# Segment 0's x: two row loads for the first 256 tokens, one DMA transpose for the rest, and Q summed per token half

## The chip, the cores and the metric

The kernel runs on one core of a Trainium2 chip. The core has five engines that run side by side, each with its own queue of instructions: TensorE (PE) multiplies matrices, VectorE (DVE) and ScalarE (ACT) work on elements, GpSimd (POOL) does masks and small copies, and SyncE (SP) here only starts transfers (DMAs). In the profile PEld are TensorE's loads of the stationary operand, which overlap its matmuls. A matmul writes to PSUM, which has 8 banks of 512 fp32 columns by 128 partitions; all other on-chip data is in SBUF. The metric is the device time of one execution in microseconds, as the median of several runs.

## The reference, cut to what matters

Two blocks read the same x (2048 tokens of 512) and are mixed by a gate per token.

```
x = A_x
g = sigmoid((x * gate_w).sum(-1, keepdims=True))
a = A(x)          # attention over 4 segments of 512 tokens, 32 heads of 16, with a memory
b = B(x)          # ((x@W_gate) * (x@W_gate > 0) * (x@W_up)) @ W_down,  512 -> 1792 -> 512
return g * a + (1 - g) * b

# A, for each segment s (q, k, v are x@wq, x@wk, x@wv):
p     = softmax(qs @ ks.T * scale + causal mask)
a_mem = (phi(qs) @ M) / (phi(qs) @ z + 1e-6)      # phi(t) = t + 1 if t > 0 else exp(t)
o     = sigmoid(beta) * a_mem + (1 - sigmoid(beta)) * (p @ vs)
M, z  = M + phi(ks).T @ vs, z + sum(phi(ks))
# out of A: o @ wo
```

## The kernel before, in words

**Layout.** Tokens are handled in four segments of L = 512. All projections need x with its 512 features on the partitions: `xT[seg % 3]` holds one segment as 4 chunks (`ci`) of 128 features by 512 tokens. For Q and K, chunk `c` of the output (128 features, 8 heads) is the sum over the four `ci` of `wq_sb[:, ci, 128c:128c+128]` (stationary) with `xT[:, ci, :]` (moving); V has x stationary and `wv_sb` moving. The gated block makes 14 tiles of 128 hidden features with the gate weights (G, `wg_sb`) and the up weights (U, `wu_sb`), and the down projection (D, `wd_sb`) sums them, together with the attention's output through `wo_sb`, into one bank per 128 tokens.

**Array shapes.** TensorE works in three shapes: full matmuls (line 493), the same matmul as four pieces of 32 output columns (line 497, used where a stretch of work holds matmuls of that shape anyway), and four row groups of 32 for the scores (line 685). P times V (line 757) and the memory update (line 880) use the pieces of 32 columns, the recall of the memory uses 32 by 32 tiles (line 855).

**Attention.** One score group (`visit`) fills four banks, or up to seven, with scores; ScalarE takes their exponential in one instruction per up to four banks (line 714), which frees the banks; GpSimd masks (line 730).

**Order.** Every step is registered with `plan.add` in the order of the program text, with an engine, a duration, a key, and what it waits for. The durations and keys are what a planner once used; at build time nothing is planned. `Plan.run` takes the numbers in `ORDER`, a written-out list of all steps, and each engine's instructions are issued in that order. `UNITS` gives the bank or buffer of each slot. `LANDS` holds assumed arrival times of the first loads in ns. Waits between engines follow from data, whatever these numbers say. Step numbers in `ORDER` count the calls of `plan.add`, so adding a step renumbers all that come later.

**The opening.** The loads at the start are issued in program text order, outside the plan, by SyncE's queue (two by ScalarE's):

- `n0` (SyncE) and `n1` (ScalarE): the first 256 features of tokens 0 to 255 and 256 to 511, rows on partitions, into `xn`;
- `q0` (SyncE), `q1` (ScalarE): `wq` for chunks 0 and 1, 128 KB each;
- on SyncE then: `ka` (`wk` chunks 0 and 1, 256 KB), `wq` chunks 2 and 3 (256 KB, line 318), the DMA transpose of the other 256 features of all 512 tokens into `xT[0][:, 2:4, :]` (line 320), `kb`, `wv`, the first pieces of `wg` and `wu`, gate_w, beta, the second pieces, the rest of `xn` for the gate (`n2`), the transpose of x for segment 1 (line 287), and the third and fourth pieces.

Meanwhile `heat` (line 1006) runs six matmuls of 512 columns and one of 128 on constants. `x0_tasks` turns chunks 0 and 1 of x on TensorE: for each chunk and each pair of token tiles, two matmuls with the identity (line 531, 128 columns each), then one copy of 256 columns to `xT[0]`, on VectorE for the first pair and on ScalarE for the second (line 546). After the last of these a matmul on zeros (`junk`, line 540, 256 columns) stands in front of Q. `proj_q` for segment 0 adds chunk by chunk, one matmul of 512 columns each: chunks 0 and 1 wait for the copies, chunks 2 and 3 for the DMA transpose. `proj_k`'s first step (chunks 0 and 1) waits for the copies and `ka`, its second for the transpose and `kb`. `load_late`, `load_xn` and `load_xT` for later segments, and the small transposes of phi(K) into `pK` (line 622) are SyncE steps within the plan.

Of the kernel before, what the change touches and what calls it, by code (L numbers as in the profile page):

```python
# [12 lines left out]
P = 128  # L13
# [179 lines left out]
def kernel(  # L193
# [71 lines left out]
    def bank(slot):  # L265
        return ps[:, slot.i * L:(slot.i + 1) * L]
# [806 lines left out]
```

## Time and profile before

| | |
|---|---|
| median of 3 runs | 262.08 us (261.82 to 262.22) |
| the profiled execution's own time | 262.61 us |
| its span, first to last instruction | 260.9 us |
| TensorE busy | 254.1 us, 97% |
| VectorE / ScalarE / GpSimd busy | 202.1 / 183.0 / 67.3 us |
| TensorE's first matmul | 0.84 us |
| first matmul of Q | 4.57 us |
| first score group | 15.27 us |

A row of the timeline gives the start, the duration, the engine, the line, the operation, output and input, shapes, and how many instructions were merged; in brackets stands the idle time of the engine just before, and what ended it. Durations of matmuls are from entry to the last result, and neighbours overlap, so the rate of a series is read from the starts. A row of the table of stretches gives the stretch, its length, busy time of each engine with the number of instructions (PE, PEld, DVE, ACT, POOL), the granted TensorE clock, the share of the DMA engines and the GB/s they moved. A few per cent of the matmul records are missing from the trace.

### The profile page before, as it was taken

The numbers are of one execution on the slowest core, as the hardware profiler recorded it, in microseconds if no ns is written. First come the engines' busy times: TensorE is split into PE (matmuls) and PEld (weight loads), VectorE is DVE, ScalarE is ACT, GpSimd is POOL, SyncE is SP. The second block draws the span as 40 slices with busy tenths as digits, with TensorE's granted clock in tenths as the row PEclk, the third lists the DMA queues.
The fourth block names the chain that finished last, engine by engine and source line by source line (L and its number), as shares of the span: only waits on it lengthen the run. The fifth ranks groups of instructions, "written<-read, shape, count | busy, mean of one in ns | idle before, by whom it ended". The sixth has DMA issues, their size and how long they took to land.

```text
span 260.9 us, 9058 instructions
## 1 busy us (share of the span) xinstructions
PE 254.1 (97%) x3914; PEld 120.7 (46%) x3942; DVE 202.1 (77%) x452; ACT 183.0 (70%) x186; POOL 67.3 (26%) x188
## 2 busy tenths in 40 slices
PE   8999999999999999999999999999999999999995
PEld 3444444444545444454545444444545444445445
DVE  2499889999888957998998894697888736596622
ACT  3199899998889678797377837989477875793000
POOL 8018742224322213113021242124112422112000
PEclk9999999999999999999999999999999999999999
DMA  7999963030006243300016541000000043000011
GB/s 194 314 284 259 283 140 105 3 68 13 3 23 132 64 114 75 68 3 3 15 35 107 167 110 57 4 0 8 14 0 10 7 145 112 0 3 3 3 40 43
DMA packets 31600, 19.75 MB, mean 76 GB/s; under 512 B 16072, under 2 KB 30024, under 8 KB 31560
## 3 DMA queue, kind: packets, MB, share of 16 engines
q1 hardware_dynamic: 31144, 18.90, 28.6%
q8 instruction: 31, 0.51, 0.9%
q10 hardware_dynamic: 416, 0.26, 0.3%
q14 instruction: 9, 0.07, 0.1%
HBM read 13.21 MB, written 2.55 MB: 60 GB/s over the span
## 4 chain that ended last, share of the span: by engine, by line
PE 97%; issue 1%; DVE 0%
PE ps L493 53%; PE ps L497 25%; PE ps L685 9%; PE ps L757 7%; PE ps L1006 1%; PE ps L880 1%; PE ps L855 0%; PE ps L531 0%; PE ps L814 0%; DVE osr L961 0%; PE ps L540 0%
## 5 line engine op out<-in xcount | busy, mean ns | idle before, releaser
L714 ACT ACTIVATE E<-ps 128x2048 bf16<-128x2048 f32 (+3 forms) x79 | 120.4, 1552 | 26.4 <-PE ps L685 25.6
L730 POOL TENSOR_SCALAR_AFFINE_SELECT E<-E 128x256 bf16<-128x256 bf16 x128 | 53.7, 448 | 155.0 <-ACT E L714 149.1
L931 DVE TENSOR_TENSOR hT<-ps,rgr 128x512 bf16<-128x512 f32 x56 | 37.8, 681 | 21.9 <-PE ps L493 13.5
L925 ACT ACTIVATE rgr<-ps 128x512 bf16<-128x512 f32 x56 | 32.7, 596 | 20.3 <-PE ps L493 11.1
L493 PE MATMUL ps<-xT,wu_sb 128*128 128x512 bf16 x158 | 41.9, 380 | 0.6 <-issue 0.5
L493 PE MATMUL ps<-xT,wg_sb 128*128 128x512 bf16 x132 | 34.9, 379 | 0.6 <-issue 0.3
L493 PE MATMUL ps<-wd_sb,hT 128*128 128x512 bf16 (+2 forms) x147 | 29.5, 339 | 1.4 <-issue 1.3
L685 PE MATMUL ps<-QT,KT 32*128 32x64 bf16 (+3 forms) x768 | 27.8, 244 | 0.0
L788 DVE STREAM_TRANSPOSE T<-ps 128x512 f32<-128x512 f32 x32 | 21.9, 701 | 3.5 <-PE ps L757 3.1
L497 PE MATMUL ps<-wd_sb,hT 128*32 128x512 bf16 x384 | 24.0, 380 | 0.0
L493 PEld LDWEIGHTS <-wu_sb 128*128 128x128 bf16 x164 | 14.9, 98 | 18.5 <-issue 2.5
L497 PE MATMUL ps<-xT,wg_sb 128*32 128x512 bf16 x344 | 23.1, 380 | 0.0
L685 PEld LDWEIGHTS <-KT 32*128 32x128 bf16 x768 | 11.0, 92 | 24.1 <-issue 22.8
L961 DVE TENSOR_SCALAR osr<-ps,ngcol 128x512 bf16<-128x512 f32 (+2 forms) x18 | 12.2, 682 | 11.3 <-PE ps L493 10.4
L493 PEld LDWEIGHTS <-wg_sb 128*128 128x128 bf16 x138 | 12.9, 98 | 15.7 <-issue 1.3
L493 PEld LDWEIGHTS <-hT 128*128 128x128 bf16 x156 | 13.5, 98 | 14.1 <-issue 2.3
L757 PE MATMUL ps<-E,Vp 128*17 128x320 bf16 (+3 forms) x512 | 19.1, 273 | 0.0
L714 ACT ACTIVATE Em<-ps 128x2048 bf16<-128x2048 f32 (+2 forms) x11 | 15.6, 1415 | 4.3 <-PE ps L685 4.1
L497 PE MATMUL ps<-xT,wu_sb 128*32 128x512 bf16 x240 | 16.2, 379 | 0.0
L588 DVE CAST QT<-ps 128x512 bf16<-128x512 f32 x16 | 10.9, 684 | 6.0 <-PE ps L493 5.5
L493 PE MATMUL ps<-xT,wq_sb 128*128 128x512 bf16 x49 | 14.3, 407 | 0.2 <-issue 0.2
L493 PE MATMUL ps<-wv_sb,xT 128*128 128x512 bf16 x54 | 13.9, 379 | 0.4 <-issue 0.3
(100 smaller groups left out, 308.7 us busy)
## 6 DMA issues: line engine op xcount, KB each, us to landing
out_dram<-osr SPq DMA_DIRECT2D x15, 128.0 KB
xn<-in_A_x_dram SPq DMA_DIRECT2D x3, 512.0 KB
xn<-coefs SPq DMA_DIRECT2D x6, 256.0 KB
cdr<-coefs SPq DMA_DIRECT2D x6, 256.0 KB
wg_sb<-in_B_W_gate_dram SPq DMA_DIRECT2D x2, 512.0 KB
wu_sb<-in_B_W_up_dram SPq DMA_DIRECT2D x2, 512.0 KB
wd_sb<-in_B_W_down_dram SPq DMA_DIRECT2D x2, 512.0 KB
wg_sb<-in_B_W_gate_dram SPq DMA_DIRECT2D x2, 384.0 KB
```

Of the source, the lines that this page charges most:

```text
L493: nc.tensor.matmul(out, lhsT=lhsT, rhs=rhs, start=start, stop=stop)
L497: nc.tensor.matmul(out[r], lhsT=lhsT[:, r], rhs=rhs, start=start, stop=stop, tile_position=(0, 32 * j))
L588: prj["q", seg, c] = plan.add("DVE", 600, key - RQK, lambda: nc.vector.tensor_copy(QT[i][:], bank(sl)), [a] + war, DVL, frees=[sl])
L685: nc.tensor.matmul(ps[:, o:o + w], lhsT=lhsT.rearrange("p h q -> p (h q)"), rhs=rhs, start=True, stop=True, tile_position=(32 * j, 0))
L714: lambda n0=n0, n1=n1, u=u, f=f, j0=j0, j1=j1: nc.scalar.activation(target(u, f, j0, j1), ps[:, banks[n0] * L:(banks[n0] + n1 - n0) * L], ...
L730: nc.gpsimd.affine_select(out=m[:, :, o:o + HP], in_=m[:, :, o:o + HP], compare_op=ALU.is_ge, fill=0.0, base=HP, pattern=[[0, 4], [1, HP]] ...
L757: nc.tensor.matmul(bank(sl)[32 * m:32 * m + HW, q:q + w], lhsT=(Vp[i] if n < 4 else Vm)[:, kb, r, 4 * c + j, 0:HW], rhs=rhs, start=(n == 0 ...
L788: done.append(plan.add("DVE", 633, key - RL, lambda r=r, sl=sl: nc.vector.transpose(T[ts.i][:, r], bank(sl)), [a] + done, 75 if r else 0, ...
L880: nc.tensor.matmul(bank(sl)[32 * j:32 * j + 32, 34 * g:34 * g + 34], lhsT=pK[i][:, t, g * P + 32 * j:g * P + 32 * j + 32], rhs=Vp[i][:, t, ...
L925: r = plan.add("ACT", 478, key - RL, lambda sl=gsl, rs=rs: nc.scalar.activation(rgr[rs.i][:], bank(sl), ACT.Relu), [g], ACL, frees=[gsl])
L931: nc.vector.tensor_tensor(hT[hs1.i][:], bank(sl), rgr[rs.i][:], ALU.mult)),
L961: nc.vector.tensor_scalar(osr[os.i][:, n0 - c0:n1 - c0], bank(sl)[:, 0:n1 - n0], ngcol[:, tt:tt + 1], None, ALU.mult)),
```

## The change

Segment 0's x is split by tokens and no longer by features. Tokens 0 to 255 come as two loads of 128 whole rows, one from each queue; TensorE turns them chunk by chunk, one matmul of 128 columns and one copy of 128 columns for each of the 4 chunks and 2 token tiles, each in a bank of its own. Tokens 256 to 511 come by one DMA transpose of all 512 features. It is issued right after `wq`'s chunks 2 and 3; `ka` moves behind it. `n2` now loads tokens 256 to 511 as rows. Q of segment 0 is summed for the first 256 tokens with one matmul of 256 columns per chunk, each waiting for that chunk's two copies, and then for the second 256 tokens in two steps of two chunks, which wait for the transpose. Both steps of K wait for the transpose. The matmul on zeros and the last warming matmul of 128 columns are gone. Some values of `LANDS` differ, and `ORDER` and `UNITS` are written anew (1377 steps for 1362).

```diff
-    LANDS = dict(n0=3470, n1=3600, q0=4640, q1=4640, ka=6350, q2=7150, q3=7150, x0=8150,
-                 kb=9000, v=10600, g0=12100, u0=13600, gw=14100, be=14400, g1=15600, u1=17100,
+    LANDS = dict(n0=3250, n1=3300, q0=4100, q1=4100, q2=5100, q3=5100, x0=6300, ka=7100,
+                 kb=8000, v=9800, g0=11300, u0=12900, gw=14100, be=14400, g1=15600, u1=17100,
...
-    halves = slice(0, D // 2), slice(D // 2, D)
-    got_n[0] = [load_x0(eng, 2 * t, 2 * t + 2, halves[0], "n%d" % t)
+    got_n[0] = [load_x0(eng, t, t + 1, slice(0, D), "n%d" % t)
                 for t, eng in enumerate((nc.sync, nc.scalar))]
...
-    got_k = [load_rows(nc.sync, wk_sb, A_wk, 0, "k")]
     nc.sync.dma_start(out=wq_sb[:, 2:NC, :],
                       in_=A_wq.rearrange("(c p) n -> p c n", p=P)[:, 2:NC, :])
-    nc.sync.dma_start_transpose(out=xT[0][:, NC // 2:NC, :], in_=x[0:L, halves[1]])
+    got_q += [arrival("q%d" % ci) for ci in range(2, NC)]
+    nc.sync.dma_start_transpose(out=xT[0][:, :, 2 * P:L], in_=x[2 * P:L, :])
     got_x0b = arrival("x0")
-    got_q += [arrival("q%d" % ci) for ci in range(2, NC)]
+    got_k = [load_rows(nc.sync, wk_sb, A_wk, 0, "k")]
...
-    got_n[0].append(load_x0(nc.sync, 0, NC, halves[1], "n2"))
+    got_n[0].append(load_x0(nc.sync, 2, NC, slice(0, D), "n2"))
...
     def x0_tasks():
...
+        for ci in range(NC):
             for t in range(2):
+                sl = plan.one("ps", (2 * ci + t,))
+                a = plan.add("PE", 107, K(-9) + 2 * ci + t, lambda t=t, ci=ci, sl=sl: nc.tensor.matmul(
+                    bank(sl)[:, 0:P], lhsT=xn[:, t, ci * P:(ci + 1) * P], rhs=ident[:],
+                    start=True, stop=True), [got_n[0][t]], PEL, need=[sl], size=2)
...
+                x0_turned[ci].append(plan.add(
+                    "ACT" if t else "DVE", 80 + (0.95 if t else 1.12) * P, K(-9) + ci,
+                    lambda t=t, ci=ci, sl=sl: (nc.scalar.copy if t else nc.vector.tensor_copy)(
+                        xT[0][:, ci, t * P:(t + 1) * P], bank(sl)[:, 0:P]), [a], DVL, frees=[sl]))
+        return [x0_turned[k] + x0_turned[k + 1] + [got_x0b] for k in (0, 2)]
...
     # proj_q, segment 0
+            for ci in range(NC):
+                a = matmuls(K(-8 + ci, c), [got_q[ci]] + x0_turned[ci], sl, [
+                    lambda ci=ci: (wq_sb[:, ci, c * P:(c + 1) * P], xT[0][:, ci, 0:2 * P])],
+                    prev=a, start=not ci, stop=ci == NC - 1, width=2 * P)
+            a = matmuls(K(-3, c), [got_x0b], sl, [
+                lambda ci=ci: (wq_sb[:, ci, c * P:(c + 1) * P], xT[0][:, ci, 2 * P:L])
+                for ci in range(NC)], prev=a, width=2 * P, at=2 * P)
...
     def heat():
-        for k in range(7):
-            w = L if k < 6 else P
+        for k in range(6):
+            w = L
...
```

In the new order TensorE runs six flips, Q of c = 1 with chunk 0, the last two flips, the other fifteen Q matmuls of the first half, five steps of the second half, and then K, the rest of Q, V, the first G and the first score group. On SyncE the plan's steps begin with the transpose of x for segment 2, two of the `wd` loads, one `pK` transpose, three `wo` loads, `xn` of segment 1 and three more `pK` transposes; before, they began with two `pK` transposes, `xn` of segment 1, one `wo` and two `wd` loads, a `pK` transpose and the transpose for segment 2.

More of the change, by code (lines that the diff above doesn't have):

```diff
@@ L31 @@
 ORDER = """
[63 rows of a table removed]
[64 rows of a table added]
 """
 UNITS = (
[L98 to L104 removed]
+    "41635207000000005201073022171036330110330000030011000003011000001001030000210102218002d013"
+    "2120b302a0110301621042205200731132231320c1129010201002202122031210013132230003011303141321"
+    "230000000000320110000023000000000200112000072010007a32263001511c11293205301012071034000262"
+    "03211b313d12280002010210721110712362231131301222317111623520310000000001200100000340110000"
+    "00230112000032010606c5123321d3006213500140201102b1138026a313902027110201700020102407231116"
+    "22011303214307046371302000000000730000000031011000000330000000670102133605b211c61220037521"
+    "9120d02043001212a114821163020025501100011021"
 )
@@ L430 @@
     got_gates = plan.add("DVE", 300, 0.0, pair_gates, got_gates, 100, lock=True)
-    att, prj, ffn, xread, x0_first = {}, {}, {}, [], []
+    att, prj, ffn, xread, x0_turned = {}, {}, {}, [], [[] for _ in range(NC)]
     UNIT, AUNIT = 16000.0, 14800.0
@@ L523, in x0_tasks @@
         plan.tag = "x0"
-        got, prev = [], None
-        for ci in range(NC // 2):
+        prev = None
+        for ci in range(NC):
             for t in range(2):
-                sl = plan.one("ps", ((4, 3, 5, 2)[2 * ci + t],))
-                def flip(t=t, ci=ci, sl=sl):
-                    for k in range(2):
-                        nc.tensor.matmul(bank(sl)[:, k * P:(k + 1) * P],
-                                         lhsT=xn[:, 2 * t + k, ci * P:(ci + 1) * P], rhs=ident[:],
-                                         start=True, stop=True)
-                a = plan.add("PE", 214, K(-9 + ci) + t, flip, [got_n[0][t]], PEL, need=[sl], size=4)
+                sl = plan.one("ps", (2 * ci + t,))
+                a = plan.add("PE", 107, K(-9) + 2 * ci + t, lambda t=t, ci=ci, sl=sl: nc.tensor.matmul(
+                    bank(sl)[:, 0:P], lhsT=xn[:, t, ci * P:(ci + 1) * P], rhs=ident[:],
+                    start=True, stop=True), [got_n[0][t]], PEL, need=[sl], size=2)
                 if prev:
@@ L537, in x0_tasks @@
                 prev = a
-                if ci == 1 and t:
-                    js = plan.one("ps", (7,))
-                    j = plan.add("PE", 214, K(-9 + ci) + t, lambda js=js: nc.tensor.matmul(
-                        bank(js)[:, 0:2 * P], lhsT=junk[:, 0:P],
-                        rhs=junk[:, None, 0:P].to_broadcast([P, 2, P]), start=True, stop=True),
-                        [a], lat=0, need=[js], frees=[js], size=2)
-                b = plan.add(
-                    "ACT" if t else "DVE", 80 + (0.95 if t else 1.12) * P * 2,
-                    K(-9 + ci), lambda t=t, ci=ci, sl=sl: (
-                        nc.scalar.copy if t else nc.vector.tensor_copy)(
-                        xT[0][:, ci, 2 * t * P:2 * (t + 1) * P], bank(sl)[:, 0:2 * P]),
-                    [a], DVL, frees=[sl])
-                got.append(b)
-        x0_first.extend([got[0:2] + [(j, 0.0)], got[2:4]])
-        return [got, [got_x0b]]
+                x0_turned[ci].append(plan.add(
[3 more added lines that the diff above has]
+        return [x0_turned[k] + x0_turned[k + 1] + [got_x0b] for k in (0, 2)]
     def proj_mm(w, c, seg):
@@ L576, in proj_q @@
             a = None
-            for ci in range(2):
-                a = matmuls(K(-8 + ci, c), [got_q[ci]] + x0_first[ci], sl, [
-                    lambda ci=ci: (wq_sb[:, ci, c * P:(c + 1) * P], xT[0][:, ci, :])],
-                    prev=a, start=not ci, stop=False)
-            for ci in range(2, NC):
-                a = matmuls(K(-6 + ci, c), [got_q[ci]] + got_x[0][1], sl,
-                            [proj_mm(wq_sb, c, 0)[ci]], prev=a, start=False, stop=ci == NC - 1)
+            for ci in range(NC):
[5 more added lines that the diff above has]
+                for ci in range(NC)], prev=a, width=2 * P, at=2 * P)
         else:
@@ L1003, in heat @@
         one = nc.const_aps.tensor(1.0, (P, 1), BF16)
-        for k in range(7):
-            w = L if k < 6 else P
+        for k in range(6):
+            w = L
             nc.tensor.matmul(bank(warm[k])[:, 0:w], lhsT=one.to_broadcast([P, P]),
                              rhs=one.to_broadcast([P, w]), start=True, stop=True)
-    plan.add("PE", 3470, -1e9, heat, lat=0, need=warm, frees=warm, size=14)
+    plan.add("PE", 3363, -1e9, heat, lat=0, need=warm, frees=warm, size=12)
     got_x[0] = x0_tasks()
```

7 lines of the change are left out of this document (removed), and 127 rows, old and new, of the table ORDER.

## The prediction

> **What bounds the kernel now.** First I read the page's busy shares and the chain that ended last, then who waited for whom on TensorE.
>
> ```profile
> span 260.9 us, 9058 instructions
> PE 254.1 (97%) x3914; PEld 120.7 (46%) x3942; DVE 202.1 (77%) x452; ACT 183.0 (70%) x186; POOL 67.3 (26%) x188
> ...
> PE 97%; issue 1%; DVE 0%
> ```
>
> The chain is TensorE from end to end. Next, the timeline of TensorE: the opening, then the first attention scores (L685).
>
> ```profile
> 0.84 2.82 PE L1006 MATMUL ps<-const-bfloat16-1.0 128*128 128x512 bf16 x7 [0.84 <-PEq L1057]
> 3.50 1.04 PE L531 MATMUL ps<-ident,xn 128*128 128x128 bf16 x8
> 4.33 0.42 PE L540 MATMUL ps<-junk 128*128 128x256 bf16 x1
> 4.57 3.00 PE L493 MATMUL ps<-xT,wq_sb 128*128 128x512 bf16 x8
> 7.41 1.89 PE L493 MATMUL ps<-xT,wk_sb 128*128 128x512 bf16 x8
> 9.13 1.03 PE L493 MATMUL ps<-xT,wq_sb 128*128 128x512 bf16 x4
> ...
> 11.94 1.89 PE L493 MATMUL ps<-wv_sb,xT 128*128 128x512 bf16 x7
> ...
> 17.34 0.59 PE L493 MATMUL ps<-xT,wu_sb 128*128 128x512 bf16 x2
> 17.86 0.40 PE L685 MATMUL ps<-QT,KT 32*128 32x448 bf16 x8
> 18.19 0.60 PE L493 MATMUL ps<-wv_sb,xT 128*128 128x512 bf16 x2
> ```
>
> From 7.41 on, eight 512-column matmuls take 9.13-7.41 = 1.72 us, 0.215 each. The first Q matmuls ran at half that rate, as their weight loads show:
>
> ```profile
> 3.50 0.77 PEld L531 LDWEIGHTS <-xn 128*128 128x128 bf16 x8 [0.42 <-DMA xn<-in_A_x_dram]
> ...
> 4.48 0.22 PEld L493 LDWEIGHTS <-wq_sb 128*128 128x128 bf16 x2
> 4.97 0.15 PEld L493 LDWEIGHTS <-wq_sb 128*128 128x128 bf16 x1 [0.28 <-issue]
> ...
> 6.25 0.15 PEld L493 LDWEIGHTS <-wq_sb 128*128 128x128 bf16 x1 [0.28 <-issue]
> 6.68 0.39 PEld L493 LDWEIGHTS <-wq_sb 128*128 128x128 bf16 x2 [0.28 <-issue]
> ```
>
> They stand 0.427 us apart (4.97 to 6.68 in four steps, two loads left out here): 1.2 columns per ns, against 2.4 later. Matmul k of the Q group starts at 4.57 + 0.427k, so the sixth starts at 6.70; K starts at 7.41, two full-rate matmuls (0.43) after the sixth's end, so the sixth took 0.28. With c us at 1.2 and 0.28-c at 2.4 columns per ns making 512 columns, c = 0.13: the clock doubled at **6.83 us**, though the granted-clock row reads full speed throughout. Before that, every us saved or lost on TensorE is worth half a us later; afterwards a whole one.
>
> Is there any waiting to remove after 7.41? TensorE's waits for others, L1006's start apart:
>
> ```profile
> PE ps L493 <- issue: 2.5, 16, 0.2
> ```
>
> The list names no engine and no transfer. The 2.5 us are mostly records that are missing, as one of eight is in the x7 row at 11.94. The score rows give the price of a change of array shape: 17.34 plus two times 0.215 is 17.77, the score starts at 17.86 (0.09 lost), and its 512 columns (0.21) end in the next start 0.33 later (0.12 lost). So the body has nothing to give but shape changes.
>
> **The change, part by part.** The sum is made against the profiled execution, 262.61 us with a span of 260.9; the median of the runs is 262.08, 0.2% lower, and I carry the difference over to that.
>
> *Warming matmuls.* The 128-column one goes, 0.11 us at 1.2 columns per ns; the six others end at 0.84 + 6 x 0.427 = 3.40. But the first flip's weight load ended its idle time on the landing of xn, at 3.50. Each row load keeps its 128 KB and its place at the head of its queue, only in 1 KB pieces. So the gain is between 0 (landing stays) and 0.11 (it lands by 3.40); nearest is the row: 0, and TensorE idles 0.10.
>
> *Flips and copies.* Eight flips stay eight, 0.107 each at the slow clock. Four copies of 256 columns become eight of 128:
>
> ```profile
> 3.94 0.85 DVE L546 CAST xT<-ps 128x256 bf16<-128x256 f32 x2 [2.32 <-PE ps L531]
> 4.15 0.80 ACT L546 CAST xT<-ps 128x256 bf16<-128x256 f32 x2 [0.99 <-PE ps L531]
> 9.84 1.29 DVE L588 CAST QT<-ps 128x512 bf16<-128x512 f32 x2 [5.05 <-PE ps L493]
> ```
>
> VectorE's take 0.42 for 256 columns and about 0.66 for 512, so some 0.29 for 128 (estimate from those two; four in a row 1.2); on ScalarE 0.28 likewise. Flip 2 starts at 3.61 and ends 0.31 later, its copy at 4.20; Q could start at 4.25. Six flips end at 4.14, so TensorE idles 0.11 where the junk matmul (0.21) stood. Nothing else is on either copying engine then: VectorE's next work was at 9.84.
>
> *The first weights and the rest of the loads.* Bytes moved, from a table of stretches:
>
> ```profile
> 0.00:3.10 3.10, 2.26 (x6) 0.87 (x7) 0.51 (x7) 1.23 (x1) 2.25 (x10) 1.00 0.29 87
> 0.00:3.90 3.90, 3.06 (x11) 1.21 (x12) 0.51 (x7) 1.28 (x1) 3.05 (x10) 1.00 0.43 138
> 0.00:4.65 4.65, 3.81 (x17) 1.86 (x18) 1.22 (x9) 1.73 (x3) 3.80 (x13) 1.00 0.53 169
> 0.00:5.45 5.45, 4.61 (x19) 2.11 (x20) 1.36 (x9) 2.03 (x3) 4.47 (x17) 1.00 0.60 193
> 5.45:6.65 1.20, 1.20 (x4) 0.40 (x3) 0.00 (x0) 0.00 (x0) 0.99 (x8) 1.00 1.26 210
> 6.65:7.55 0.90, 0.90 (x5) 0.45 (x4) 0.00 (x0) 0.00 (x0) 0.00 (x0) 1.00 1.12 300
> 0.00:3.41 3.41, 2.57 (x7) 0.87 (x7) 0.51 (x7) 1.28 (x1) 2.56 (x10) 1.00 0.36 110
> 3.41:6.83 3.42, 3.42 (x17) 1.79 (x16) 0.85 (x2) 0.74 (x2) 2.89 (x15) 1.00 1.11 291
> ```
>
> The last column is GB/s. 270 KB (both xn loads) were through at 3.10 and seen at 3.50: a lag of 0.40. 538 KB (with q0 and q1) were through at 3.90, so q0 lands at 4.30; the weight load at 4.48 bounds it above. The first Q starts at 4.30 (bounds 4.25 and 4.48), after 0.16 of idling.
>
> Then one Q (0.213), two flips (0.213), and at 4.73 fifteen more Q of 256 columns: 9.85 of them by 6.83, the other 5.15 at 0.108 take 0.56. The first half of Q, 4096 columns, ends at **7.39**. Before, the same 4096 columns were done at 7.41. Gain 0.02; with the bounds (xn at 3.40 and Q at 4.16; or Q at 4.48) between 0.09 gained and 0.07 lost.
>
> *The other half by DMA.* The transpose loses the 256 KB of wk ahead of it:
>
> ```profile
> 2.29 0.47 SPq L318 DMA_DIRECT2D wq_sb<-in_A_wq_dram  x1
> 2.81 1.33 SPq L320 DMA_TRANSPOSE xT<-in_A_x_dram  x1
> ```
>
> It is issued from 2.30 to 3.63. Ahead of it stand 786 KB instead of 1052 KB: through at 4.65 instead of 5.45, and its own 256 KB at the 210 GB/s row's 1.2 us end at 5.85; with the lag, 6.25. The other end: the trace proves it only by its use at 9.13 (weights at 8.92), so 0.80 earlier 8.12 or even 8.33. Nearest is the measured lag: 6.25, 1.1 us before its need at 7.39. The change makes it needed sooner, for K's first chunks no longer run without it; so this cover is what hides it. The wq chunks 2 and 3 land at 5.05 for a seventh Q at 5.79; wk's first half, moved behind the transpose, at 5.85 + 0.90 + 0.40 = 7.15 for about 8.47; its second at 8.05 for 9.3. From wv on the same bytes stand ahead.
>
> *Halved matmuls.* Q of segment 0 becomes 32 matmuls of 256 instead of 16 of 512. At full speed, at the end of the kernel:
>
> ```profile
> 256.67 0.60 PE L493 MATMUL ps<-wo_sb,oT 128*128 128x256 bf16 x4
> ...
> 257.10 0.33 PE L493 MATMUL ps<-wd_sb,hT 128*128 128x128 bf16 x3
> ```
>
> Four take 0.43, 0.108 each, half of 0.215: cost 0, bounds 0 and 0.04. The Trainium skill's "TensorE: Matmul & The Clock Gate", section "Back-to-back issue gap", adds 2.5 ns to each warm matmul: 16 more would make the sum 0.04 us worse. The rows show no more than that, and the measurement decides.
>
> *The written-out order.* Decoded, both lists have 63 score groups, 3 recalls and 23 stretches between them that start in 32-column tiles: as many shape changes, so 0. On SyncE's queue the transpose of x for segment 2 moves from behind the first pK transposes to the very front, with two wd loads; the pK transposes and segment 1's xn stand behind them. That xn feeds only gate work, whose first step stands behind segment 1's first K copies on VectorE.
>
> ```profile
> 10.75 6.95 SPq L287 DMA_TRANSPOSE xT<-in_A_x_dram  x1
> ...
> 21.30 2.87 SPq L622 DMA_TRANSPOSE pK<-pkT  x2
> ...
> 34.16 1.38 SPq L287 DMA_TRANSPOSE xT<-in_A_x_dram  x1
> ```
>
> Such a transpose held the queue 1.38 us when quiet and 6.95 when full, so pK slips from 21.3 to between 24 and 30. Its first reader is the memory update at
>
> ```profile
> 60.04 0.67 PE L880 MATMUL ps<-Vp,pK 128*32 128x34 bf16 x64
> ```
>
> so it is covered 30 us; without that cover it would cost up to those 7. The tail ends in the same 128-column pieces and one store: 0.
>
> **Sum:** -0.02 us, bounds -0.09 and +0.11: 262.06, say **262.1**.
>
> **Rivals.**
>
> *A, the clock comes later (slower).* The stretch 3.41 to 6.83 was busy without a break (3.42 of 3.42) and ended in the faster clock; 0 to 3.41 was busy 2.57 of 3.41, 75%, and didn't. The new opening has holes of 0.10 and 0.16 in the second: 92% busy. If such a stretch must be nearer to full, the clock rises one stretch later, at 10.24: 3.41 us at 1.2 instead of 2.4 columns per ns is 1.7 us, **263.8**. For it: the 75% that failed. Against: 92% is nearer to 100. It decides between 75 and 92. The Trainium skill's page named above, section "What's actually happening", speaks of a free-running window of about 3.4 us that must be busy; the trace's 3.41 fits, and no run here yet shows how busy.
>
> *B, the transposed half is late.* At the far end (8.12) TensorE stands 0.73 at full rate: **262.8**. Against: the lag of xn.
>
> *C, the new order has waits.* ScalarE's exponentials free the banks of the next score:
>
> ```profile
> 18.32 1.88 ACT L714 ACTIVATE E<-ps 128x2048 bf16<-128x2048 f32 x1 [0.23 <-PE ps L685]
> ...
> 20.91 1.88 ACT L714 ACTIVATE E<-ps 128x2048 bf16<-128x2048 f32 x1 [0.18 <-PE ps L685]
> ```
>
> The margins are 0.2 us, and the new order has other work between scores. Five scores late by 0.2: **263.1**. For it: 1377 steps are placed anew. Against: the old order has no such wait.
>
> *D, the clock comes earlier (faster).* Where those stretches begin may differ between executions; the first full one could end at 0.84 + 3.41 = 4.25, worth (6.83-4.25)/2 = 1.3 us: **260.8**. For 0.2% it must move 1.0 us. Against: nothing in the change does it, and three runs lie 0.4 us apart.
>
> **How the numbers follow.** From no change, 0.2% (0.52 us: 261.56 to 262.60) is about what a measurement can tell. Forecast 0.42; A 0.20; B 0.08; C 0.16; D 0.14. So faster 0.14, same 0.42, slower 0.44. The forecast's own range is 261.6 to 262.6. The range to hold 8 in 10 goes from 261.5 (leaving out most of D) to 263.9 (taking in A).
>
> **What would show it.** Right: Q's last first-half matmul near 7.4, the second half following without a gap, weight loads 0.213 apart until about 6.8, first score near 13.9 instead of 15.27 (30 matmuls' worth of 0.215 stand between it and 7.39, and 0.09), no transfer named in TensorE's waits. Wrong: slow spacing past 7 us (A), a hole before the second half (B), idle time of TensorE before scores (C), the fast spacing before 6 us (D).

## The result and the profile after

The changed kernel takes 262.77 us in the median (262.31 to 263.17), the kernel before 262.08 us on the same chip (261.59 to 262.46). The ratio is 1.0028, with a 95% interval of 1.0016 to 1.0041: slower by 0.4 to 1.1 us. The profiled execution is one of the quicker ones: 262.35 us, with a span of 260.6.

The page of the changed kernel, its busy shares and the chain that ended last:

```profile
span 260.6 us, 9198 instructions
PE 256.4 (98%) x3998; PEld 121.2 (46%) x3998; DVE 202.4 (78%) x454; ACT 183.1 (70%) x188; POOL 66.8 (26%) x188
...
PE 95%; DMA 2%; SPq 1%; issue 0%; DVE 0%
PE ps L493 52%; PE ps L497 26%; PE ps L671 9%; PE ps L743 7%; DMA wk_sb<-in_A_wk_dram 2%; PE ps L866 1%; SPq L320 1%; SPq L281 1%; PE ps L841 0%; PE ps L800 0%; SPq L317 0%; DVE osr L947 0%
```

TensorE is still nearly the whole chain, but 2% of it now lie on a transfer, the load of wk. The opening, in the timeline of TensorE (flips are L528, scores L671 here):

```profile
3.76 0.64 PE L528 MATMUL ps<-ident,xn 128*128 128x128 bf16 x6 [0.20 <-DMA xn<-in_A_x_dram]
4.52 0.27 PE L493 MATMUL ps<-xT,wq_sb 128*128 128x256 bf16 x1
4.63 0.27 PE L528 MATMUL ps<-ident,xn 128*128 128x128 bf16 x2
4.74 3.08 PE L493 MATMUL ps<-xT,wq_sb 128*128 128x256 bf16 x25
7.72 1.04 PE L493 MATMUL ps<-xT,wk_sb 128*128 128x512 bf16 x4
9.05 1.04 PE L493 MATMUL ps<-xT,wk_sb 128*128 128x512 bf16 x4 [0.29 <-DMA wk_sb<-in_A_wk_dram]
...
13.69 0.40 PE L671 MATMUL ps<-QT,KT 32*128 32x448 bf16 x8
```

Two things differ from the forecast. First, the clock: six flips take 0.64 us from the first start to the last end; in the second profile below, at the slow clock, the same six take 0.90. Within the row the starts stand 0.056 apart from 4.01 on, where the second profile has 0.107. So the clock doubled by 4.0, some 2.8 us earlier than in the profiled execution of before. Second, the early clock brought little, for the loads are late. TensorE's waits by the list:

```profile
PE ps L493 <- DMA wk_sb<-in_A_wk_dram: 0.3, 1, 0.3
PE ps L528 <- DMA xn<-in_A_x_dram: 0.2, 1, 0.2
```

That is not all. The wait for a weight falls on the weight load, so the timeline of PEld shows more (in brackets its idle time and what ended it):

```profile
5.46 2.08 PEld L493 LDWEIGHTS <-wq_sb 128*128 128x128 bf16 x20 [0.29 <-DMA wq_sb<-in_A_wq_dram]
7.71 0.55 PEld L493 LDWEIGHTS <-wk_sb 128*128 128x128 bf16 x4 [0.17 <-DMA wk_sb<-in_A_wk_dram]
9.04 0.55 PEld L493 LDWEIGHTS <-wk_sb 128*128 128x128 bf16 x4 [0.78 <-DMA wk_sb<-in_A_wk_dram]
```

A weight load can run one matmul ahead, so the brackets are not what TensorE lost; that is read from the starts of its matmuls. The sixth Q of the first half after the flips could have started at 5.29 and started at 5.46: 0.18 lost on wq's chunks 2 and 3. K could have started at 7.66 and started at 7.72: 0.06 on wk's first half. Its second four could have started at 8.59 and started at 9.05: 0.46 on wk's second half. Together 0.70 us. From the first Q at 4.52 to the first score stand two flips, 32 matmuls of 256 columns at 0.109 and 22 of 512 columns at 0.216 (12 of K, 8 of V, 2 of G), with the change of shape (0.09) 8.44 us: the score would have come at 12.96. With the 0.70 it is 13.66; measured 13.69. So the opening is accounted for to 0.1 us.

When had the bytes of each load moved? Stretches from the start of the span (columns as before the change, the last is GB/s):

```profile
0.00:4.55 4.55, 3.38 (x13) 1.22 (x14) 1.04 (x10) 1.63 (x4) 3.71 (x13) 1.00 0.51 173
0.00:6.70 6.70, 5.52 (x32) 2.91 (x33) 1.53 (x11) 2.15 (x5) 5.46 (x24) 1.00 0.73 197
0.00:7.50 7.50, 6.32 (x39) 3.62 (x40) 1.61 (x12) 2.15 (x5) 5.46 (x24) 1.00 0.77 210
```

787, 1320 and 1575 KB: what stands up to wq's chunks 2 and 3, up to wk's first half, and up to its second half (786, 1310 and 1573 KB). They were seen at 5.46, 7.71 and 9.04, so 0.9, 1.0 and 1.5 us after as many bytes had moved; the forecast took the 0.40 of the first load for all.

As many bytes are not the load's own, though. The trace keeps sixteen marks of arrival for each of these loads, and wherever TensorE waited for one, it went on 0.04 to 0.05 us after the last mark. In us from the start of the span:

| | wq, chunks 2 and 3 | transpose of x | wk, first half | wk, second half | wv |
|---|---|---|---|---|---|
| forecast | 5.05 | 6.25 | 7.15 | 8.05 | |
| this profile, twelfth mark | 5.38 | 6.40 | 7.16 | 7.85 | 9.80 |
| this profile, last mark | 5.42 | 6.44 | 7.67 | 9.00 | 10.43 |
| eight profiles with the change's order of loads, last mark | 5.42 to 5.94 | 6.44 to 6.97 | 7.67 to 9.32 | 9.00 to 10.07 | 10.43 to 11.58 |
| four profiles with the order of before, last mark | 5.94 to 6.38 | 6.94 to 7.44 | 5.19 to 5.66 | 7.96 to 8.20 | 9.78 to 10.89 |

(Some of these profiles belong to the runs below.) Most of wk was there when the forecast had it; the last few of the sixteen were not. And wk's second half has the same bytes ahead of it in both orders, yet is complete 0.8 to 2.1 us later in the change's: what counts is not the bytes ahead alone.

**A second profile of both kernels, unchanged.** Theories from here on: L, the loads of the opening make the difference, and the clock's doubling moves from one execution to the next in both kernels; X, the row loads of 1 KB pieces land 0.25 us later every time; H, the holes in TensorE's opening delay the clock.

> The changed kernel once more, unaltered: a second execution to read. Theory L (loads set the start): the moment at which the TensorE clock doubles moves between executions (6.83 us in the one of before, about 4.3 in the one of after), and when it comes early the changed kernel has to wait for wk (waits of about 0.2 to 0.8 us for it, second half near 9.05), so its fastest runs stand near 262.3 and its slowest, with the clock at 7 us or later, near 263.1. Theory X (the row loads): xn lands near 3.75 again, 0.25 later than before, and every run pays the same 0.2 to 0.3 us for it whatever the clock does; the spread of the runs is then as wide as that of the kernel before. Theory H (the hole delays the clock): the clock doubles later than 7 us in most executions.

> The kernel before, unaltered: a second execution to read. Theory L: if the clock doubles early in this execution (before 6 us) K follows Q at once without any wait for a load, the first score comes near 14.2 to 14.5 us instead of 15.27, and the time is near 261.6; with a clock rise near 6.8 it is 262.5 again. Fastest runs near 261.5. Theory X: xn lands near 3.50 again. Theory H: the clock never doubles later than about 7 us.

Measured: 262.51 us (262.00 to 263.42; 1.0018, 1.0005 to 1.0031) for the changed kernel, 262.14 (261.37 to 262.56; 0.9997, 0.9984 to 1.0009) for the kernel before, and 262.18 for the kernel before beside them. In this profiled execution of the changed kernel the clock doubled late, at about 6.8, as the forecast had supposed. Its weight loads:

```profile
5.91 2.50 PEld L493 LDWEIGHTS <-wq_sb 128*128 128x128 bf16 x20 [0.42 <-DMA wq_sb<-in_A_wq_dram]
8.43 0.64 PEld L493 LDWEIGHTS <-wk_sb 128*128 128x128 bf16 x4
9.51 0.55 PEld L493 LDWEIGHTS <-wk_sb 128*128 128x128 bf16 x4 [0.45 <-DMA wk_sb<-in_A_wk_dram]
```

and its flips and first score, in the timeline of TensorE:

```profile
3.49 0.90 PE L528 MATMUL ps<-ident,xn 128*128 128x128 bf16 x6
...
14.16 0.40 PE L671 MATMUL ps<-QT,KT 32*128 32x448 bf16 x8
```

This is the forecast's own case: K at 8.43 to 8.54 where it had 8.47, but wq's chunks 2 and 3 at 5.91 (it had 5.05) and wk's second half at 9.51 (it had 8.05, needed at 9.3); the score at 14.16 instead of 13.9. By the starts of its matmuls TensorE lost 0.15 and 0.12 us to the two loads. The list of waits named no transfer at all here.

The kernel before, second profile, had the early clock:

```profile
4.56 1.96 PE L493 MATMUL ps<-xT,wq_sb 128*128 128x512 bf16 x8
6.36 1.89 PE L493 MATMUL ps<-xT,wk_sb 128*128 128x512 bf16 x8
8.08 1.03 PE L493 MATMUL ps<-xT,wq_sb 128*128 128x512 bf16 x4
...
10.94 1.90 PE L493 MATMUL ps<-wv_sb,xT 128*128 128x512 bf16 x8
...
14.28 0.40 PE L685 MATMUL ps<-QT,KT 32*128 32x448 bf16 x8
```

Eight Q matmuls took 6.36-4.56 = 1.80 us instead of 2.84: at 0.215 each but for the first, the clock doubled near 4.7. No load up to wk is waited for. The first score is 1.0 us earlier than in the first profile (15.27), and then some of it goes:

```profile
PE ps L685 <- ACT E L714: 0.4, 1, 0.4
PE ps L493 <- DMA xT<-in_A_x_dram: 0.2, 1, 0.2
```

ScalarE's exponentials and the next segment's x can't follow as early. L had put such an execution near 261.6; it took 262.44. No execution of the kernel before near its fastest times, 261.4 to 261.7, was profiled, so that those are the ones with the early clock is likely, not shown. So X falls (the first flip came at 3.47 and 3.50 in the kernel before, at 3.49 and 3.76 in the changed one, and at 3.38 to 3.67 in its variants), and H falls: 6.83 and 4.7 in one kernel, 4.0 and 6.8 in the other. The Trainium skill, "TensorE: Matmul & The Clock Gate", section "What's actually happening", says that the window of about 3.4 us runs freely and that the transition therefore moves by 0.5 us either way; the traces agree that it moves, but over 4.0 to 6.8, more than twice as far.

### The profile page after: what moved, and what is told of

Same layout as the page of the kernel before. It is cut to its first block, busy times and chain, and to the rows that moved or that the text cites. A ratio compares the mean times of both kernels' runs of the same rounds, so it can differ in the third digit from the quotient of the medians.

```text
span 260.6 us, 9198 instructions
## 1 busy us (share of the span) xinstructions
PE 256.4 (98%) x3998; PEld 121.2 (46%) x3998; DVE 202.4 (78%) x454; ACT 183.1 (70%) x188; POOL 66.8 (26%) x188
## 4 chain that ended last, share of the span: by engine, by line
PE 95%; DMA 2%; SPq 1%; issue 0%; DVE 0%
PE ps L493 52%; PE ps L497 26%; PE ps L671 9%; PE ps L743 7%; DMA wk_sb<-in_A_wk_dram 2%; PE ps L866 1%; SPq L320 1%; SPq L281 1%; PE ps L841 0%; PE ps L800 0%; SPq L317 0%; DVE osr L947 0%
## 5 line engine op out<-in xcount | busy, mean ns | idle before, releaser
L493 PE MATMUL ps<-xT,wu_sb 128*128 128x512 bf16 x164 | 41.1, 380 | 0.0
L493 PE MATMUL ps<-xT,wg_sb 128*128 128x512 bf16 x142 | 37.0, 380 | 0.0
L493 PE MATMUL ps<-wd_sb,hT 128*128 128x512 bf16 (+2 forms) x150 | 30.1, 340 | 0.0
L671 PE MATMUL ps<-QT,KT 32*128 32x64 bf16 (+3 forms) x768 | 27.8, 244 | 0.0
L497 PE MATMUL ps<-wd_sb,hT 128*32 128x512 bf16 x408 | 25.2, 380 | 0.0
L671 PEld LDWEIGHTS <-KT 32*128 32x128 bf16 x768 | 11.0, 92 | 24.3 <-issue 23.3
L497 PE MATMUL ps<-xT,wg_sb 128*32 128x512 bf16 x328 | 21.6, 380 | 0.0
L493 PEld LDWEIGHTS <-hT 128*128 128x128 bf16 x150 | 12.9, 98 | 13.1 <-issue 2.3
L592 DVE CAST ktr<-ps 128x512 bf16<-128x512 f32 x16 | 11.0, 689 | 6.6 <-PE ps L493 5.7
L497 PEld LDWEIGHTS <-hT 128*32 128x32 bf16 x408 | 9.9, 97 | 9.4 <-issue 1.1
```

The costliest lines, as they stand in the source:

```text
L493: nc.tensor.matmul(out, lhsT=lhsT, rhs=rhs, start=start, stop=stop)
L497: nc.tensor.matmul(out[r], lhsT=lhsT[:, r], rhs=rhs, start=start, stop=stop, tile_position=(0, 32 * j))
L592: d = plan.add("DVE", 600, key - RQK, lambda: nc.vector.tensor_copy(ktr[ks.i][:], bank(sl)), [a], DVL + 40, need=[ks], frees=[sl])
L671: nc.tensor.matmul(ps[:, o:o + w], lhsT=lhsT.rearrange("p h q -> p (h q)"), rhs=rhs, start=True, stop=True, tile_position=(32 * j, 0))
```

## Is the rest of the kernel the same?

For each of the 63 score groups I took its start and subtracted the durations of all TensorE steps that stand ahead of it in the order; the zero is set so that the same number at the last group means the same end, whichever order. A number is then how late the kernel is at that point ("own time" is the time of the profiled execution):

```
                    own time   at score 0   at score 4   own time - score 4
before                262.61      +0.02        +0.02          262.59
before_again          262.44      -0.97        -0.14          262.58
before_ka_late        263.11      +0.53        +0.53          262.58
before_x1_early       262.11      -0.98        -0.48          262.59
before_no_w_wait      262.54      -0.04        -0.04          262.58
after                 262.35      -0.25        -0.25          262.60
after_again           262.83      +0.22        +0.22          262.61
after_q_first         262.73      +0.13        +0.12          262.61
after_no_q_wait       262.66      +0.06        +0.06          262.60
after_no_w_wait       262.17      -0.43        -0.44          262.61
after_no_w_again      262.30      -0.32        -0.33          262.63
after_no_x_wait       262.77      +0.15        +0.14          262.63
after_ka_first        263.28      +0.65        +0.65          262.63
after_q2_act          263.07      +0.10        +0.09          262.98
```

In all but the last the own time is 262.58 to 262.63 plus what the fifth score group shows. (The last loses another 0.3 at a later group; I did not find by what.) So both orders take the same from there on, to 0.05 us, and the difference is made in the first 26 us. The two first profiles say the same without the table, the tail included: from the first Q to the end of the span, before has 260.9 - 4.57 us less 1.13 for the slow clock, after 260.6 - 4.52 less the 0.70 lost and 0.11 for two flips; that is 255.2 and 255.3.

## The experiments

**One move alone, in the kernel before.** wk's first half goes behind the DMA transpose, nothing else.

```diff
-    got_k = [load_rows(nc.sync, wk_sb, A_wk, 0, "k")]
+    got_k = [arrival("ka")]
...
     nc.sync.dma_start_transpose(out=xT[0][:, NC // 2:NC, :], in_=x[0:L, halves[1]])
+    nc.sync.dma_start(out=wk_sb[:, 0:2, :],
+                      in_=A_wk.rearrange("(c p) n -> p c n", p=P)[:, 0:2, :])
```

> The kernel before with one part of the change alone: the first half of wk is loaded behind the transpose instead of ahead of it. Everything else as before. Theory L: the first eight K matmuls now wait for it, it lands near 7.7 us; executions with an early clock lose up to 1.4 us, those with a late one 0.3, so the median goes up by 0.6 to 0.9 us (262.7 to 263.0), and the fastest run stands near 262.8. Theories X and H: no row load and no gap in front of Q is touched, so it stays within 0.2 us of the kernel before.

Measured: 263.47 us (263.11 to 263.55, five executions), 1.0047 (1.0031 to 1.0063), more than L gave. The weight loads of its profiled execution:

```profile
6.33 0.59 PEld L495 LDWEIGHTS <-wq_sb 128*128 128x128 bf16 x3 [0.27 <-issue]
7.90 0.55 PEld L495 LDWEIGHTS <-wk_sb 128*128 128x128 bf16 x4 [0.97 <-DMA wk_sb<-in_A_wk_dram]
```

The move costs 1.3 us in the median. In this execution, whose clock doubled near 6.4, wk came at 7.90 where Q had ended near 7.25. wk's second half, with as many bytes ahead as before, was complete only at 9.10. In the kernel before this one move costs for certain. The changed kernel loses less; that its order has the second half of two Q chunks ahead of K would explain it, but no run tests that.

**More Q ahead of K.** In the changed kernel, the steps with the remaining second halves of Q move ahead of K.

```diff
-    117 44 99 ... 7 119 122 8 ... 78 103 77 ... 107 120 108 ... 10 104 140 141 105 ...
+    117 44 99 ... 7 119 103 104 120 122 8 ... 78 77 ... 107 108 ... 10 140 141 105 ...
```

> The changed kernel with three steps of the written-out TensorE order moved: the rest of Q's second half (six matmuls of 256 columns, 0.65 us) runs ahead of K, so that wk is needed 0.65 us later. Loads as in the changed kernel. Theory L: in executions with an early clock the waits for wk shrink or go, and the fastest runs come down by about 0.5 us to 261.8; late-clock runs stay (263.1); the median falls by 0.2 to 0.4 us. Theories X and H: no change beyond 0.1 us.

Measured: 262.75 us (262.05 to 263.45), 1.0024 (1.0012 to 1.0036): no gain over the change, where L gave 0.2 to 0.4 us.

```profile
5.99 3.01 PE L493 MATMUL ps<-xT,wq_sb 128*128 128x256 bf16 x26 [0.55 <-DMA wq_sb<-in_A_wq_dram]
8.84 2.75 PE L493 MATMUL ps<-xT,wk_sb 128*128 128x512 bf16 x12
11.43 2.00 PE L493 MATMUL ps<-wv_sb,xT 128*128 128x512 bf16 x8
13.54 0.59 PE L493 MATMUL ps<-xT,wg_sb 128*128 128x512 bf16 x2
```

The wait for wk is gone. But wq's chunks 2 and 3 came at 5.99 in this execution (0.71 lost, for the matmul could have started at 5.28), and eight V matmuls, 1.72 us of work, took from 11.43 to 13.54: 0.39 lost on what comes next. The two holes ended with a copy of K on VectorE (line 592) and a copy of V on ScalarE (line 623), not with a transfer.

**Without the wait for wq's chunks 2 and 3.** Segment 0's first halves of Q use chunks 0 and 1 of wq in their place: the same matmuls, another Q.

```diff
-                    lambda ci=ci: (wq_sb[:, ci, c * P:(c + 1) * P], xT[0][:, ci, 0:2 * P])],
+                    lambda ci=ci: (wq_sb[:, ci % 2, c * P:(c + 1) * P], xT[0][:, ci, 0:2 * P])],
```

> The changed kernel, where the first half of Q (tokens 0 to 255) multiplies chunks 2 and 3 with the weights of chunks 0 and 1, which are there already; so the load of wq's chunks 2 and 3, which still runs, is waited for only by the second half. (Q's first half is thereby another product than the reference's.) Theory L (the loads set the opening), in its form after the last runs: the seventh Q matmul waits for that load (it ended idle times at 5.46, 5.91 and 5.99), which costs 0.3 to 0.5 us of TensorE; with an early clock the wait for wk at 9.0 to 9.5 then takes its place, with a late one it is a gain of some 0.2 us. Median 0.1 to 0.3 us below the changed kernel, about 262.4. If the loads do not matter: no change from 262.6.

Measured: 262.68 us (262.00 to 263.37), 1.0025 (1.0013 to 1.0037): nothing gained, where L gave 0.1 to 0.3 us; taken alone this is what was expected if the loads did not matter. The profiled execution had the late clock (about 6.8) and lost only 0.02 us at wk. That an execution with an early clock stands at wk for longer in exchange is likely, not shown.

**Without the waits for wq's chunks 2 and 3 and for wk.** As above, and segment 0's K uses wq in place of wk, in two runs. Segment 0's K is another too. The second halves of Q still read wq's chunks 2 and 3; neither trace has a wait there.

```diff
+    k0 = lambda c: [lambda ci=ci: (wq_sb[:, ci % 2, c * P:(c + 1) * P], xT[0][:, ci, :]) for ci in range(NC)]
-        a = matmuls(key, [(w, 0.25) for w in war if w], sl, proj_mm(wk_sb, c, seg),
+        a = matmuls(key, [(w, 0.25) for w in war if w], sl, proj_mm(wk_sb, c, seg) if seg else k0(c),
```

> As after_no_q_wait, and K of segment 0 is multiplied with wq's chunks 0 and 1 instead of wk, whose loads still run; so neither is waited for, and the opening hangs on the row loads, the transposed half, wv and the clock. (K of segment 0 is another product too.) Theory L: the whole loss against the kernel before goes: median 262.0 to 262.2, fastest runs 261.5. If the loss came from the halved matmuls, the order behind the opening or the hole before the flips: it stays at 262.5 or more.

> The changed kernel without waits for weights once more, beside the run without the wait for the transposed half on the same chip. Y and Z alike: 262.29 as before, 262.2 to 262.4; where it comes to 262.1 or less, the 0.2 us left was scatter.

Measured: 262.29 us (262.08 to 262.49; L gave 262.0 to 262.2), 1.0012 (1.0003 to 1.0021), and 262.33 (262.08 to 262.77), 1.0012 (1.0003 to 1.0020). TensorE runs through, and the spread shrinks from 0.9 to 1.4 us to 0.4 to 0.7:

```profile
4.74 6.46 PE L493 MATMUL ps<-xT,wq_sb 128*128 128x256 bf16 x41
11.04 1.03 PE L493 MATMUL ps<-wv_sb,xT 128*128 128x512 bf16 x4
...
13.51 0.40 PE L671 MATMUL ps<-QT,KT 32*128 32x448 bf16 x8
```

By the ratios to the kernel before, 1.0028 and 1.0018 for the changed kernel and 1.0012 in both runs without these waits, the weights' waits cost 0.16 to 0.42 us (0.0006 to 0.0016 of 262), and 0.3 us (0.0012) is left. The intervals overlap, so the shares are rough. All executions taken together say it more firmly: the 20 of the changed kernel lie 0.61 us above the mean of the kernel before beside them, the 24 without the waits 0.25; the difference is 0.36, with a standard error of about 0.12. The upper end moves too: 263.17 and 263.42 with the waits, 262.49 and 262.77 without. In the two profiles the clock doubled near 5.9 and 6.0, and V, at 11.04 and 11.15, began 0.07 and 0.04 us after wv's last mark.

**The same in the kernel before.**

```diff
-                            [proj_mm(wq_sb, c, 0)[ci]], prev=a, start=False, stop=ci == NC - 1)
+                            [lambda ci=ci: (wq_sb[:, ci % 2, c * P:(c + 1) * P], xT[0][:, ci, :])], prev=a, start=False, stop=ci == NC - 1)
```

and K as in the diff above.

> The kernel before, where segment 0's Q uses wq's chunks 0 and 1 in place of 2 and 3, and its K uses wq's chunks 0 and 1 in place of wk (same matmuls, wrong Q and K of segment 0): no matmul ahead of V waits for wk or for wq's chunks 2 and 3. It is the same edit as in the run of the changed kernel without waits for weights (262.29). L, the loads alone make the difference: the kernel before waits for none of these weights in its traces, so it stays at 262.0 to 262.2, and the 0.2 us that the changed kernel keeps without waits is something else. S, executions of the kernel before with the early clock lose time to weights too: the median falls to 261.5 to 261.8, and its slowest execution stays below 262.4.

Measured: 262.10 us (261.61 to 262.58), 0.9999 (0.9988 to 1.0010). The kernel before loses nothing to these weights: L, not S.

**wk's first half back ahead of the transpose, in the changed kernel.**

```diff
+    nc.sync.dma_start(out=wk_sb[:, 0:2, :], in_=A_wk.rearrange("(c p) n -> p c n", p=P)[:, 0:2, :])
     nc.sync.dma_start_transpose(out=xT[0][:, :, 2 * P:L], in_=x[2 * P:L, :])
-    got_x0b = arrival("x0")
-    got_k = [load_rows(nc.sync, wk_sb, A_wk, 0, "k")]
+    got_x0b, got_k = arrival("x0"), [arrival("ka")]
```

> The changed kernel with wk's first half issued ahead of the DMA transpose, behind wq's chunks 2 and 3, as the kernel before has it. L: no wait for wk's first half is left (worth 0.2 to 0.5 us where it showed), but the transposed half has 256 KB more ahead of it, some 0.85 us at 300 GB/s, and lands near 7.3 instead of at or before 6.5, where Q's second half is to start between 6.6 and 7.4: it waits 0 to 0.7 us. So 262.3 to 263.0, with the transpose or nothing named in place of wk. Rival T, the transposed half lands early enough either way: 262.1 to 262.3 and no wait before K.

Measured: 263.01 us (262.49 to 264.67), 1.0037 (1.0021 to 1.0053), the upper end of what L gave.

```profile
6.24 1.27 PE L493 MATMUL ps<-xT,wq_sb 128*128 128x256 bf16 x10 [0.21 <-DMA wq_sb<-in_A_wq_dram]
8.01 1.25 PE L493 MATMUL ps<-xT,wq_sb 128*128 128x256 bf16 x10 [0.50 <-DMA xT<-in_A_x_dram]
9.10 1.89 PE L493 MATMUL ps<-xT,wk_sb 128*128 128x512 bf16 x8
```

wk is not waited for; the transposed half is, until 8.01. Ten halved matmuls of 0.108 from 6.24 on end at 7.32, so 0.69 us of TensorE's work is lost there. By the marks it was complete at 7.96, against 6.44 to 6.97 with the change's order of loads, so 1.0 to 1.5 us later. Not all of that need be the 256 KB: wq's chunks 2 and 3, with the same loads ahead as in the change, were complete only at 6.20 in this execution. wk's second half came at 8.73, earlier than in any of the eight. So neither place for wk's first half is free: the change gives its transpose a need of 6.5 to 7.4, which the kernel before puts at 9.13 and, with the early clock, at 8.08.

**wq's chunks 2 and 3 in two loads on two queues.**

```diff
-    nc.sync.dma_start(out=wq_sb[:, 2:NC, :],
-                      in_=A_wq.rearrange("(c p) n -> p c n", p=P)[:, 2:NC, :])
-    got_q += [arrival("q%d" % ci) for ci in range(2, NC)]
+    got_q += [load_wq(nc.scalar, 2),
+              load_wq(nc.sync, 3)]
```

> The changed kernel, where wq's chunk 2 is loaded by ScalarE's queue and chunk 3 by SyncE's, 128 KB each, instead of both in one load of SyncE's. Nothing is left out. Theory L: chunk 2 lands up to half a us earlier than 5.5 to 6.0, so part of the gain of after_no_q_wait, 0.1 to 0.2 us; the transposed half and wk come no earlier. If all 16 engines simply move the same bytes in the same order: no change.

Measured: 262.74 us (262.14 to 264.64), 1.0035 (1.0018 to 1.0051), no gain.

```profile
5.92 2.08 PEld L493 LDWEIGHTS <-wq_sb 128*128 128x128 bf16 x20 [0.34 <-DMA wq_sb<-in_A_wq_dram]
8.53 0.54 PEld L493 LDWEIGHTS <-wk_sb 128*128 128x128 bf16 x4 [0.53 <-DMA wk_sb<-in_A_wk_dram]
```

Chunk 2 came no earlier (5.92 against 5.46 and 5.91). The Trainium skill, "DMA: Bandwidth & Descriptors", section "Issuing engines are not separate DMA queues", says that loads of several engines share the same 16 DMA engines, so that a second issuer saves only issue time; the run agrees.

**No wait for any load ahead of V.** On top of the run without waits for weights, Q's second half reads the first 256 tokens again, and K has wq as its moving operand too.

```diff
-                lambda ci=ci: (wq_sb[:, ci, c * P:(c + 1) * P], xT[0][:, ci, 2 * P:L])
+                lambda ci=ci: (wq_sb[:, ci % 2, c * P:(c + 1) * P], xT[0][:, ci, 0:2 * P])
```

> The changed kernel with no matmul of segment 0 ahead of V waiting for any load but the two row loads and wq's chunks 0 and 1: beside the replaced weights, Q's second half reads tokens 0 to 255 again and K has 512 columns of wq as its moving operand (same matmuls, wrong Q and K of segment 0). Y, the 0.2 us left without waits for weights is the transposed half, waited for when the clock doubles early: the median falls to the kernel before's 262.1 or below it, and the fastest to 261.4 to 261.7. Z, the transposed half is never waited for and the 0.2 us lies elsewhere: 262.2 to 262.4, as without waits for weights, and the fastest stays at 262.0.

Measured: 262.38 us (261.73 to 262.77), 1.0006 (0.9996 to 1.0016). The median is as Z has it, the fastest nearer to Y; neither is settled. The profiled execution had the early clock (25 halved matmuls from 4.82 to 7.54), and yet ended at 262.77:

```profile
4.82 2.89 PE L493 MATMUL ps<-xT,wq_sb 128*128 128x256 bf16 x25
...
11.62 1.02 PE L493 MATMUL ps<-wv_sb,xT 128*128 128x512 bf16 x4 [0.89 <-DMA wv_sb<-in_A_wv_dram]
```

The next load in the queue, wv, holds TensorE now, for 0.89 us by the list and 1.05 by the starts (two Q matmuls from 10.35 on end at 10.57). Whatever this execution gained ahead of it ended there.

**A try at a faster kernel.** The early clock's lead of 1.0 us in the kernel before was partly lost on segment 1's x; so its transpose is issued earlier.

```diff
+    load_xT(1)
     load_gu(1)
...
-    load_xT(1)
```

> The kernel before with one transfer moved: the transpose of x for segment 1 is issued ahead of the second pieces of the gate and up weights instead of behind them and n2. In before_again TensorE had 1.0 us in hand at the first score (early clock) and lost 0.8 of it by the fourth, with a wait that ended on that transpose. Theory L: executions with an early clock keep that lead, so the fastest runs and the median come down, by 0.2 to 0.4 us in the median (261.8 to 262.0); late-clock runs stay at 262.6. If the lead is lost elsewhere (ScalarE's exponentials): no change.

Measured: 262.49 us (262.03 to 263.43), 1.0020 (1.0008 to 1.0032): slower by 0.4 us, against what was hoped for.

```profile
PE ps L493 <- DVE hT L931: 0.3, 1, 0.3
```

The profiled execution kept 0.48 of its lead, and lost the rest waiting for VectorE's `hT` (line 931). By its one profile alone it would be a gain (262.11); the median says otherwise. What the other executions lose was not seen. No version beat the kernel before.

## Why the prediction was right and wrong

262.77 lies within the range (261.5 to 263.9), 0.7 us above the forecast of 262.1 and outside the forecast's own range (261.6 to 262.6); slower by over 0.2% had the largest chance, 0.44, but for other reasons than the one that decided. The range reached that far for the prices of rivals A, B and C, none of which came true, so that it held the time was luck as far as the mechanism goes.

- *Warming matmuls, flips and copies, 0:* right. Q's first matmul came at 4.52, with xn 0.26 later than supposed, and at 4.21 to 4.50 in the other runs of the changed order; the forecast took 4.30.
- *The lag of the loads, 0.40 for all:* **this step failed.** wq's chunks 2 and 3 were given 5.05 and were complete at 5.42 to 5.94 in the eight profiles with the change's order of loads; wk's first half was given 7.15 and was complete at 7.67 to 9.32, its second 8.05 and 9.00 to 10.07. After as many bytes the lag measured 0.9 to 1.5, and it doesn't follow from the bytes: for wk's second half 8.05 was right in the order of before (7.96 to 8.20), and moving the first half behind the transpose made the second 0.8 us and more later with the same bytes ahead, in the kernel before as well (9.10). Twelve of the sixteen marks were there by 7.2 to 7.7 and 7.9 to 8.4; why the last few come so late in this order is open. The margins that follow from the forecast's times (0.74, 1.3 and 1.25 us) were smaller than that error together with the next. "From wv on the same bytes stand ahead" fell by the same step: wv came at 10.43 to 11.58 for 9.78 to 10.89.
- *One moment for the clock, 6.83:* the second size that was off. The sum priced one execution's opening, while the doubling moves from 4.0 to 6.8 over the profiles, in both kernels by over 2 us. Rival D had the mechanism, but took it for a gain of the changed kernel. The kernel before can use an early clock as far as its scores, for it waits for none of these weights (262.10 without them); the changed kernel can't. So the loads cost most where the clock is early: 0.70 us in the first profile, of the 1.2 that the early clock was worth from the first Q on ((6.83 - 4.52)/2).
- *The transposed half, 6.25 (rival B):* complete at 6.44 to 6.97, so later than forecast, but right in what hangs on it: it was in time wherever the order of loads was the change's, in the first profile by 0.1 us. (The trace of before has its transposed half complete at 7.44; less the forecast's 0.80 that is 6.64.) B's kind of mechanism decided, with other transfers.
- *Halved matmuls, 0:* right: 25 of them from 4.82 to 7.54 are 0.109 each, against 0.108. Over all the openings the starts of halved matmuls stand 109.1 ns apart and those of whole ones 215.8, so two halves take 2.5 ns more than a whole. That bears out the sentence on the issue gap: 0.04 us for the 16, too little to see in the median.
- *The new order, SyncE's queue and the tail, 0 (rival C):* right; the table of score groups leaves them less than 0.05 us.
- *Rival A, the clock comes later:* wrong; never later than 6.9 in any trace, holes or not. The 3.41 us of its stretches was half of 6.83, so that it fitted said nothing, and the other moments don't keep to stretches counted from the start of the span.
- *What would show it:* "no transfer named in TensorE's waits" was a bad sign to look for: in one profile the list named none, and the weight loads had waited 0.42 and 0.45 (0.15 and 0.12 on TensorE).

Open is some 0.25 to 0.3 us of the median, which stays without waits for weights. The wait for wv in one profile, and wv's last mark just ahead of V in the two without waits for weights, suggest that the later loads of the opening take it from executions with an early clock; that isn't shown for the median.

## What to carry to other kernels

Price a load that is moved, and the loads behind it, by when the last part of a load arrives in such an order, not by the bytes ahead and the lag of the first load, and test the margin for the earliest clock as well as for the latest. Where several loads arrive one just behind the other, taking away the wait for one need give nothing: two such runs left the time as it was (more Q ahead of K, no wait for wq), one lost, and only all weights together gained. A weight that is late can show at the weight load alone and not in the list of TensorE's waits; what it costs is read from the starts of the matmuls.

## What the runs showed of the hardware

The doubling of the clock moved between executions of the same program: 4.0 and 6.8 us in two profiles of the changed kernel, 6.8 and 4.7 in two of the kernel before. A load was complete only with the last of its sixteen marks: twelve of wk's second half were there by 8.09 in one profile and the last at 10.07, and TensorE went on 0.04 to 0.05 us after the last one. With the same bytes ahead, that half was complete at 7.96 to 8.20 where the DMA transpose stood right ahead of it (four profiles), and at 9.00 to 10.07 where wk's first half stood between them (eight). With 256 KB more ahead of it, the DMA transpose of the changed kernel was complete at 7.96 instead of 6.44 to 6.97, where 256 KB at the 300 GB/s of the stretch from 6.65 to 7.55 of the kernel before are 0.87 us; that is one execution. In the kernel before, 256 KB fewer ahead left it at 7.09, within its 6.94 to 7.44, also in one.
